# A spectral mixer and a gated feed-forward on one core: moving operands read alternately from their two halves

## The chip, the core and the metric

The kernel runs on one core of a Trainium2 chip. The metric is the device time of one execution in microseconds (us). The engines are named as the profile names them: PE is TensorE, the matrix engine; PEld is its weight load, which runs beside the matmuls; DVE is VectorE, ACT is ScalarE, POOL is GpSimd, SP is SyncE, which issues most DMAs. A matmul has a stationary operand (the weights, at most 128 x 128) and a moving operand, whose columns stream past the weights into PSUM. SBUF is the on-chip memory that both come from.

## What is computed

Two tensors are mixed by a gate: a spectral layer over 4096 tokens of width 640, and a gated feed-forward on the same tokens.

```python
x = A_x                                       # [2, 1, 4096, 640], fp32
g = sigmoid((x * gate_w).sum(-1, keepdims=True))
Xf = rfft2(x, axes=(1, 2))                    # over the 4096 tokens
z = Xf.reshape(B, H, Wf, 4, 160)              # four blocks of 160 channels
h = relu(z @ w1 + b1)                         # complex, by block
o = softshrink(h @ w2 + b2, 0.01)             # complex, by block
a = irfft2(o)
b = (gelu(x @ w_gate) * (x @ w_up)) @ w_down  # 640 -> 1728 -> 640
return g * a + (1 - g) * b
```

## The kernel before

All products run on PE in a 4-byte float format (fp32r) that carries part of a float's mantissa. Each float operand is therefore kept as two parts: `high` (L277) writes the rounded part with ACT, `low` (L280) the remainder with DVE, and a product takes three matmuls: high times high, high times low, low times high. A second transform of the spectral part (`fwd2`, L978) uses plain fp32 instead, which the profile records as two matmuls each.

The program goes through these stages, with one instruction order that is written out by hand for all engines:

- **Gate and up products** (`quad` L582, `deep_parts` L681, `plain` L730, `mixed` L762). Token tiles of 512 are the moving operand, in halves of 256 columns; weights of 128 x 128 are stationary. The products use a scheme with fewer multiplications (sums and differences of blocks), once for pairs and in part twice. All their matmuls go through `run` (L560, matmul on L562), through `go` in `deep_parts` (L694), or through L744 in `plain`. Between the products, hooks slip in the work of other stages: the first transform of the spectral part (`a_step`, L806, matmul on L817, 320 columns), the preparation of weights, and DMAs.
- **Spectral part.** For each chunk of 256 frequencies (one chunk has 258) and each of four blocks: `fwd2` makes the second step of the transform, `mlp1` (L1044) and `mlp2` (L1104) the two layers, `y_split` (L1129) and `inv1` (L1140) the first step of the way back. Its matmuls go through `mms` (L295, matmul on L297) and L1064 to L1066. In `mlp1` the moving operands are the transformed chunks `z`, `zs` and `zl` (256 columns), in `mlp2` the weights of the second layer (320 columns), in `inv1` the split output `ys` (320 columns).
- **Down product** (`down`, L1378), for 32 groups of tokens. The activations are stationary, the 640-wide weights are moving, 320 columns each. Its matmuls stand on L1406 (two products interleaved, `duo`) and on L562. `inv2` (L1351) makes the last step of the way back and feeds its result into the same output rows.

Every one of these matmuls loads new weights, so PEld has one record for each PE record. The addresses in SBUF come from pools with a fixed size for each kind of tile. Several tiles have gaps or offsets inside (`xs` in L518, `s2s` in L1299, `wx` in L1283).

The lines that the change touches are the matmuls themselves (L297, L562, L694, L744, L817, L1064 to L1066, L1406), the order of columns that `fwd2` writes to PSUM (L983) and what reads it (L984 to L1002), the shape of `y` in `mlp2` (L1110, L1124) and `y_split` (L1133, L1137), and the layouts that the host makes in `_tables` and `_layouts`. The rest of `quad` and `down` is the same in both kernels.

Of the kernel before, what the change touches and what calls it, by code (L numbers as in the profile page):

```python
# [15 lines left out]
P = 128  # L16
# [26 lines left out]
def _tables():  # L43
# [39 lines left out]
    f2 = np.concatenate([f2[0].reshape(P, P), f2[1].reshape(P, P), fny.reshape(P, 8)], axis=1)  # L83

    k2e = np.concatenate([np.arange(16), 31 - np.arange(16)])
    sig = np.concatenate([np.ones(16), -np.ones(16)])
# [128 lines left out]
def spectral_mix_kernel(ctx: ExitStack, tc: tile.TileContext, a):  # L215
# [79 lines left out]
    def mms(dst, ops):  # L295
        for i, (l, r) in enumerate(ops):
            nc.tensor.matmul(dst, l, r, start=i == 0, stop=i == len(ops) - 1)  # L297

# [258 lines left out]

    def run(dst, ops, first=True):  # L560
        for i, (l, r) in enumerate(ops):
            nc.tensor.matmul(dst, l, r, start=first and i == 0, stop=i == len(ops) - 1, skip_group_check=True)  # L562
            while inner and i == 1:
                inner.pop()()

# [115 lines left out]
    def deep_parts(gr, tp, t):  # L681
# [7 lines left out]
        def go(m, n, first, dst):  # L689
            if n not in b:  # L690
                b[n] = bank()
            acc = b[n][:, :256]
            for i, (l, r) in enumerate(prod([wa[m]], [xa[m]])):
                nc.tensor.matmul(acc, l, r, start=first and i == 0, stop=i == 2, skip_group_check=True)  # L694
            nc.vector.tensor_add(dst, acc, dst)

        def f0():
# [32 lines left out]
    def plain(key, t, hook):  # L730
# [3 lines left out]
        if t == 0:  # L734
            x = [x_of(o, *n, ("k4", q)) for q, n in enumerate((("b11", "b21"), ("b12", "b22")))]
            n = {}
            for q, ks, pause in ((0, (0, 1), (0, 1, 1)), (0, (2, 3), (5, 1, 0)), (0, (4,), (0,) * 3), (1, (4,), (0,) * 3),
                                 (1, (0, 1), (0,) * 3), (1, (2, 3), (0,) * 3)):
                for (a_, b_), z in zip(((0, 0), (1, 0), (0, 1)), pause):
                    warm(z)  # L740
                    for g, (dst, w) in enumerate(((pg, w0), (pu, w1))):
                        for i in ks:
                            m = n[q, g] = n.get((q, g), 0) + 1
                            nc.tensor.matmul(dst[:, 256 * q:256 * q + 256], w[:, i, a_], x[q][i][b_], start=m == 1,  # L744
                                             stop=m == 15, skip_group_check=True)
            for k in range(7):
                hook(k)
# [58 lines left out]
    def a_step(b, n2, h):  # L806
# [7 lines left out]
        for q in range(2):  # L814
            cs = slice(320 * q, 320 * q + 320)
            pa = bank()
            nc.tensor.matmul(pa[:, :320], f[:, h], xs[:, cs], start=True, stop=True)  # L817
# [160 lines left out]
    def fwd2(b, c, o, z, zs=None):  # L978

        pz = bank()  # L980
        for kp in range(4):
            ft = F2[0][:, 0:P] if (c == 0 and kp == 0) else F2[0][:, P:2 * P]
            nc.tensor.matmul(pz[:, kp * P:(kp + 1) * P], SC[b, c, kp][:, o:o + P], ft, start=True, stop=True)  # L983
        zz = [z[h][:, :, :CH].rearrange("p r (k f) -> p r k f", k=4) for h in range(2)]  # L984
        pr = pz.rearrange("p (k r f) -> p r k f", k=4, r=2)
        high(zz[0], pr)
        if zs:
            t = part_of(b, c, 0)
            t4 = t[:, :CH].rearrange("p (k f) -> p k f", k=4)
            nc.scalar.activation(t4, pr[:, 1], AF.Copy)  # L990
        low(zz[1], pr, zz[0])
        if zs:
# [1 line left out]
        if wide(b, c):  # L994
            pn = bank()
            for q in range(2):
                nc.tensor.matmul(pn[:, :4], SC[q, c, 0][:, o:o + P], fny[:, 4 * q:4 * q + 4], start=q == 0, stop=q == 1)
            split(z[0][:, :, CH:], z[1][:, :, CH:], pn[:, :4].rearrange("p (r f) -> p r f", r=2))
            if zs:
                nc.vector.tensor_copy(t[:, CH:], pn[:, :2])  # L1000
        F = width(b, c)
        return lambda: split(zs[0][:, :F], zs[1][:, :F], t[:, :F])  # L1002

    def rest(b, c):
# [39 lines left out]
    def mlp1(b, c, n, sums):  # L1044
# [15 lines left out]
        def last(dst):  # L1060

            for r in range(2):
                k = LAST1[r]
                nc.tensor.matmul(dst, w[:, k:k + P], z[0][:, r], start=r == 0, stop=False, skip_group_check=True)  # L1064
                nc.tensor.matmul(dst, w[:, k:k + P], z[1][:, r], start=False, stop=False, skip_group_check=True)  # L1065
            nc.tensor.matmul(dst, wl[:, 256:384], t1[:, n, :F], start=False, stop=True, skip_group_check=True)  # L1066
        h = two(b, c, "h")
        if wide(b, c):
            if n < 2:
# [34 lines left out]
    def mlp2(b, c, n):  # L1104
# [2 lines left out]
        q = n % 2  # L1107
        for j, (f0, M) in enumerate([(0, P), (P, P)] + ([(CH, 2)] if wide(b, c) else [])):
            if q == 0:
                Y[b, c, n // 2, j] = small([P, 2, 2, BS], name="y")  # L1110
            y = Y[b, c, n // 2, j]
            py = bank()
            fs = slice(f0, f0 + M)
# [1 line left out]
            for r in range(2):  # L1115
# [5 lines left out]

            m = small([P, 320], name="m")
            nc.scalar.activation(m[:M], py[:M, :320], AF.Relu, bias=neg2lam[:M])
            nc.vector.scalar_tensor_tensor(y[:M, :, q], py[:M, :320].rearrange("p (r o) -> p r o", r=2), 0.0,  # L1124
                                           m[:M].rearrange("p (r o) -> p r o", r=2), op0=OP.min, op1=OP.add)

    YS = {}

    def y_split(b, c, pb):  # L1129
        if wide(b, c):  # L1130
            t = NY[pb] = small([P, 2, 320], F32R, name="ny")
            nc.gpsimd.memset(t.bitcast(F32), 0.0)
            split(t[:2, 0], t[:2, 1], Y.pop((b, c, pb, 2))[:2, 0].rearrange("p n o -> p (n o)"))  # L1133
        for j in range(2):
            y = Y.pop((b, c, pb, j))
            t = YS[b, c, pb, j] = big([P, 2, 2, 320], F32R, name="ys")
            split(t[:, 0], t[:, 1], y.rearrange("p r n o -> p r (n o)"),  # L1137
                  nc.gpsimd if j == 1 and (b, c, pb) < (1, NCH - 2, 1) else nc.vector)

    def inv1(b, c, pb):  # L1140
# [237 lines left out]
    def down(i, u, hooks):  # L1378
# [18 lines left out]
        def duo(X, x, Y, y, hook, more=False):  # L1397
# [4 lines left out]
            for j, (p, q) in enumerate(zip(hx, hy)):  # L1402
                if j == 4:
                    hook()
                for k, op in ((0, p[0]), (0, p[1]), (1, q[0]), (0, p[2]), (1, q[-1]), *([(1, q[1])] if len(q) == 3 else ())):
                    nc.tensor.matmul((X, Y)[k], *op, start=n[k] == 0 and not (more and k), stop=n[k] == tot[k] - 1,  # L1406
                                     skip_group_check=True)
                    n[k] += 1

# [370 lines left out]
```

## Time and profile before

| | before |
|---|---|
| median of 3 runs | 2533.25 us (2531.83 to 2545.23) |
| span of the profiled execution | 2529.7 us |
| instructions in it | 54653 |
| PE records: L562 with 256 columns | 11196 |
| PE records: L1406 with 320 columns | 3844 |
| PE records of all kinds | 20239 |
| mean DMA rate over the span | 197 GB/s |

The profile comes from one execution. Its span runs from the first instruction to the last. The profile's page gives the busy time of each engine, the clock that the throttle granted to PE, the chain of work that ended last (followed back from the last instruction), and groups of equal instructions. Other views are cut from the same trace: busy time by windows of the span, with the number of instructions that start there; the chain in order of time, where one row is a run of equal instructions with its start, its length and its count; and the instructions of one engine in order of time, merged in rows of the same kind. Matmuls overlap, so the duration of one is longer than the distance from one to the next.

### The profile page before, as it was taken

What the parts mean: (1) busy time and instruction counts of PE and PEld (TensorE: products, weight loads), DVE (VectorE), ACT (ScalarE), POOL (GpSimd) and SP (SyncE); (2) the same over time, 40 slices, a digit from 0 to 9 for tenths busy, and PEclk for the clock granted to TensorE, in tenths of its full rate; (3) what the DMA queues carried; (4) which work ended last, traced back from release to release, by engine and by line L of the source; (5) the groups of instructions that cost most, each with busy time, mean ns of one, the idle gap of its engine ahead of it and who ended that gap; (6) DMA issues with size and microseconds to landing.
All of it is one profiled execution on the core that took longest, in us unless ns stands there. A gap on an engine that the chain in (4) does not pass through costs nothing.

```text
span 2529.7 us, 54653 instructions
## 1 busy us (share of the span) xinstructions
PE 2522.0 (100%) x20239; PEld 2516.3 (99%) x20239; DVE 2078.9 (82%) x4323; ACT 1492.6 (59%) x3503; POOL 387.3 (15%) x404
## 2 busy tenths in 40 slices
PE   9999999999999999999999999999999999999999
PEld 9999999999999999999999999999999999999999
DVE  7677788777777877787668788888999999899998
ACT  5455456656656666666556778787644444444443
POOL 0111100000000000000003111111133333333332
PEclk9999999999999999999999999999999999999999
DMA  6566666777777677777667455548744444444432
GB/s 216 203 214 229 224 224 211 245 234 241 234 251 236 220 235 243 237 239 227 217 228 220 130 164 142 161 144 270 289 142 147 157 157 140 133 152 157 154 131 102
DMA packets 351422, 499.50 MB, mean 197 GB/s; under 512 B 26028, under 2 KB 223276, under 8 KB 351156
## 3 DMA queue, kind: packets, MB, share of 16 engines
q1 hardware_dynamic: 333684, 445.02, 54.6%
q0 software_dynamic: 17472, 51.00, 5.5%
q8 instruction: 159, 2.61, 0.4%
q14 instruction: 107, 0.88, 0.1%
HBM read 307.10 MB, written 188.81 MB: 196 GB/s over the span
## 4 chain that ended last, share of the span: by engine, by line
PE 95%; DVE 2%; DMA 2%; ACT 1%; issue 0%; SPq 0%; DVEq 0%; ACTq 0%
PE bank L562 52%; PE bank L1406 22%; PE bank L297 14%; PE bank L983 3%; PE bank L694 2%; PE bank L817 1%; PE bank L1064 1%; PE bank L1065 1%; DMA xraw<-in_xT_dram 0%; DMA wdf<-wf 0%; PE bank L1066 0%; DMA scr<-as 0%; DMA zl<-zl 0%; DVE xo L281 0%; DMA wx<-wdf 0%
## 5 line engine op out<-in xcount | busy, mean ns | idle before, releaser
L562 PE MATMUL bank<-xo,w 128*128 128x256 f32 x11196 | 1319.4, 277 | 1.6 <-ACT u L588 0.6
L562 PEld LDWEIGHTS bank<-xo,w 128*128 128x128 f32 x11196 | 1298.0, 188 | 3.4 <-ACT u L588 1.2
L1406 PE MATMUL bank<-wx,ho 128*128 128x320 f32 x3844 | 560.7, 306 | 0.0
L1406 PEld LDWEIGHTS bank<-wx,ho 128*128 128x128 f32 x3844 | 557.2, 187 | 0.0
L281 DVE TENSOR_TENSOR ho<-hraw,ho 128x640 fp32r<-128x640 f32 (+3 forms) x384 | 260.8, 720 | 23.1 <-ACT ho L278 20.2
L588 ACT ACTIVATE u<-bank 128x256 f32<-128x256 f32 x328 | 125.5, 383 | 174.6 <-PE bank L562 166.4
L278 ACT ACTIVATE ho<-hraw 128x640 fp32r<-128x640 f32 x320 | 167.1, 571 | 97.7 <-PE bank L1406 74.9
L281 DVE TENSOR_TENSOR xs<-xr,xs 64x640 fp32r<-64x640 f32 x128 | 105.0, 820 | 75.8 <-ACT xs L278 73.6
L640 DVE TENSOR_TENSOR u<-bank,u 128x256 f32<-128x256 f32 x204 | 85.9, 421 | 86.4 <-ACT u L588 85.5
L281 DVE TENSOR_TENSOR xo<-xraw,xo 128x512 fp32r<-128x512 f32 x194 | 133.2, 687 | 16.4 <-ACT xo L278 15.1
L297 PE MATMUL bank<-wm,h 128*128 128x320 f32 (+1 forms) x792 | 137.6, 309 | 0.0
L819 DVE TENSOR_TENSOR as<-bank,as 64x320 f32<-64x320 f32 x256 | 113.9, 484 | 21.8 <-ACT as L818 20.1
L278 ACT ACTIVATE xo<-xraw 128x512 fp32r<-128x512 f32 x194 | 121.6, 627 | 6.1 <-DMA xraw<-in_xT_dram 4.9
L297 PEld LDWEIGHTS bank<-wm,h 128*128 128x128 f32 (+1 forms) x792 | 117.9, 185 | 1.3
L588 ACT ACTIVATE p<-bank 128x256 f32<-128x256 f32 x144 | 55.2, 383 | 105.8 <-DVE h L651 54.6
L562 PE MATMUL bank<-wx,ho 128*128 128x320 f32 x764 | 116.3, 307 | 0.0
L562 PEld LDWEIGHTS bank<-wx,ho 128*128 128x128 f32 x764 | 112.0, 188 | 0.0
L818 ACT ACTIVATE as<-bank 64x320 f32<-64x320 f32 x256 | 96.7, 426 | 23.8 <-PE bank L817 20.3
L278 ACT ACTIVATE xs<-xr 64x640 fp32r<-64x640 f32 x128 | 94.0, 734 | 22.9 <-DMA xr<-in_x_dram 21.1
L278 ACT ACTIVATE ho<-hs 128x640 fp32r<-128x640 f32 (+1 forms) x128 | 68.5, 570 | 61.5 <-DVE ho L281 42.1
L770 POOL MEMSET h<- 64x512 f32 x16 | 8.4, 523 | 624.9 <-PE bank L817 249.1
L1373 ACT ACTIVATE uu<-bank,gs 128x320 f32<-128x320 f32 x120 | 54.7, 524 | 76.5 <-PE bank L297 76.0
(196 smaller groups left out, 3961.8 us busy)
## 6 DMA issues: line engine op xcount, KB each, us to landing
xo<-xD SPq DMA_DIRECT2D x124, 512.0 KB
xraw<-in_xT_dram SPq DMA_DIRECT2D x215, 256.0 KB
hD<-h SPq DMA_DIRECT2D x184, 256.0 KB
hraw<-hD SPq DMA_DIRECT2D x128, 320.0 KB
xD<-xo POOLq DMA_DIRECT2D x64, 512.0 KB, 3.6
sc<-scr SPq DMA_DIRECT2D x65, 320.0 KB
xr<-in_x_dram SPq DMA_DIRECT2D x64, 320.0 KB
scr<-as SPq DMA_DIRECT2D x64, 320.0 KB
```

The lines of the kernel that those rows point to most:

```text
L278: nc.scalar.activation(dst, src, AF.Copy, scale=scale)
L281: eng.tensor_sub(dst, src, hi.bitcast(F32))
L297: nc.tensor.matmul(dst, l, r, start=i == 0, stop=i == len(ops) - 1)
L562: nc.tensor.matmul(dst, l, r, start=first and i == 0, stop=i == len(ops) - 1, skip_group_check=True)
L588: copy = lambda d, s_: nc.scalar.activation(d, s_, AF.Copy)
L640: nc.vector.tensor_add(u4, C, u4)
L694: nc.tensor.matmul(acc, l, r, start=first and i == 0, stop=i == 2, skip_group_check=True)
L818: nc.scalar.activation(stg[hi, cs], pa[lo, :320], AF.Copy)
L819: nc.vector.tensor_add(stg[hi, cs], pa[hi, :320], stg[hi, cs])
L983: nc.tensor.matmul(pz[:, kp * P:(kp + 1) * P], SC[b, c, kp][:, o:o + P], ft, start=True, stop=True)
L1373: nc.scalar.activation(uu[n2][:, cs], pe[:, :320], AF.Copy, scale=gs[:, b, 0, n2:n2 + 1])
L1406: nc.tensor.matmul((X, Y)[k], *op, start=n[k] == 0 and not (more and k), stop=n[k] == tot[k] - 1, skip_group_check=True)
```

## The change

Each fp32r moving operand with n columns is read in the order 0, n/2, 1, n/2+1, and so on. A helper gives the matmul a view of the same bytes with two steps:

```diff
+    def by_two(m):
+        return m.rearrange("p (k i) -> p i k", k=2)
...
     def mms(dst, ops):
         for i, (l, r) in enumerate(ops):
-            nc.tensor.matmul(dst, l, r, start=i == 0, stop=i == len(ops) - 1)
+            nc.tensor.matmul(dst, l, by_two(r), start=i == 0, stop=i == len(ops) - 1)
...
     def run(dst, ops, first=True):
         for i, (l, r) in enumerate(ops):
-            nc.tensor.matmul(dst, l, r, start=first and i == 0, stop=i == len(ops) - 1, skip_group_check=True)
+            nc.tensor.matmul(dst, l, by_two(r), start=first and i == 0, stop=i == len(ops) - 1, skip_group_check=True)
...
-            nc.tensor.matmul(pa[:, :320], f[:, h], xs[:, cs], start=True, stop=True)
+            nc.tensor.matmul(pa[:, :320], f[:, h], by_two(xs[:, cs]), start=True, stop=True)
...
-                for k, op in ((0, p[0]), (0, p[1]), (1, q[0]), (0, p[2]), (1, q[-1]), *([(1, q[1])] if len(q) == 3 else ())):
-                    nc.tensor.matmul((X, Y)[k], *op, start=n[k] == 0 and not (more and k), stop=n[k] == tot[k] - 1,
+                for k, (l, r) in ((0, p[0]), (0, p[1]), (1, q[0]), (0, p[2]), (1, q[-1]), *([(1, q[1])] if len(q) == 3 else ())):
+                    nc.tensor.matmul((X, Y)[k], l, by_two(r), start=n[k] == 0 and not (more and k), stop=n[k] == tot[k] - 1,
```

The matmuls on L694, L744 and L1064 to L1066 change in the same way. The warm-up matmuls at the start (L1516) and the plain fp32 ones (L983, L997) keep their moving order.

The results now come out in the alternated order, so the data are laid out to fit. On the host, `apart` puts the channels of the input, the token tiles, and the columns of the down weights in the order that the read undoes, and the columns of the second layer are permuted twice over, since its output is a moving operand again later. The columns of the second transform's table (`f2`) are reordered to match:

```diff
+    def apart(a, n):
+        return a.reshape(*a.shape[:-1], -1, n // 2, 2).swapaxes(-1, -2).reshape(a.shape)
+    perm = apart(perm, 320)
...
-    xp = xt.reshape(16, 2, 256, 5, P).transpose(0, 4, 1, 3, 2)
+    xp = apart(xt.reshape(16, 2, 256, 5, P).transpose(0, 4, 1, 3, 2), 256)
...
-    o["wd"] = c(A("B_w_down"))
+    o["wd"] = c(apart(A("B_w_down"), 320))
...
+    four = np.arange(BS).reshape(40, 2, 2).transpose(1, 2, 0).reshape(-1)
+    w2, b2 = w2[..., four], b2[..., four]
```

On the chip, `fwd2` writes its four products to PSUM in runs of 32 columns, so that the frequencies stand in the order that `mlp1` reads; and `mlp2` reads its result from PSUM with a step of two (real and imaginary parts alternate) and writes `y` in runs of 40:

```diff
-            nc.tensor.matmul(pz[:, kp * P:(kp + 1) * P], SC[b, c, kp][:, o:o + P], ft, start=True, stop=True)
-        zz = [z[h][:, :, :CH].rearrange("p r (k f) -> p r k f", k=4) for h in range(2)]
-        pr = pz.rearrange("p (k r f) -> p r k f", k=4, r=2)
+            nc.tensor.matmul(pz.rearrange("p (r e k f) -> p k r e f", r=2, e=2, k=4)[:, kp], SC[b, c, kp][:, o:o + P],
+                             ft.rearrange("p (r e f) -> p r e f", r=2, e=2), start=True, stop=True)
+        F = width(b, c)
+        if F > CH:
+            zz = [z[h][:, :, :F].rearrange("p r (e n) -> p r e n", e=2)[..., :P] for h in range(2)]
+            pr = pz.rearrange("p (r e n) -> p r e n", r=2, e=2)
+        else:
+            zz, pr = [z[h][:, :, :F] for h in range(2)], pz.rearrange("p (r n) -> p r n", r=2)
...
-                Y[b, c, n // 2, j] = small([P, 2, 2, BS], name="y")
+                Y[b, c, n // 2, j] = small([P, 2, 4, 2, 40], name="y")
...
-            nc.vector.scalar_tensor_tensor(y[:M, :, q], py[:M, :320].rearrange("p (r o) -> p r o", r=2), 0.0,
-                                           m[:M].rearrange("p (r o) -> p r o", r=2), op0=OP.min, op1=OP.add)
+            nc.vector.scalar_tensor_tensor(y[:M, :, :, q], py[:M, :320].rearrange("p (m n r) -> p r m n", m=4, r=2), 0.0,
+                                           m[:M].rearrange("p (m n r) -> p r m n", m=4, r=2), op0=OP.min, op1=OP.add)
```

No instruction is added, removed or moved on any engine. Only access patterns differ, and an access pattern shows in the order of instructions by its shape alone. On PE, in the spectral part, between the last matmuls of one `mlp1` and the sums of the next (`f` is the table of the second transform, `sc` its input, `wm` and `wl` the weights of the first layer, `z`, `zs` and `zl` its inputs), there stood before:

```order
L1066 MATMUL bank<-zl_20085,wl 128x256
L983 MATMUL bank<-f_19590,sc 128x128 x4
L997 MATMUL bank<-fny,sc 128x4 x2
L983 MATMUL bank<-f_19590,sc 128x128 x4
L297 MATMUL bank<-zs,wm 128x256 x3
L297 MATMUL bank<-z,wm 128x256 x3
```

At the same place there stands now:

```order
L1081 MATMUL bank<-zl_20085,wl 128x256
L993 MATMUL bank<-f_19590,sc 128x4x32 x4
L1012 MATMUL bank<-fny,sc 128x4 x2
L993 MATMUL bank<-f_19590,sc 128x4x32 x4
L307 MATMUL bank<-zs,wm 128x256 x3
L307 MATMUL bank<-z,wm 128x256 x3
```

The second transform's matmuls write four runs of 32 columns each; the others stand as they were, and their alternated reading is on the input side, which these rows don't print.

More of the change, by code (lines that the diff above doesn't have):

```diff
@@ L82, in _tables @@
     fny[:, 0, :, 0, 0] = fny[:, 0, :, 1, 1] = (-1.0) ** n2
-    f2 = np.concatenate([f2[0].reshape(P, P), f2[1].reshape(P, P), fny.reshape(P, 8)], axis=1)
+    f2 = [t.reshape(P, 2, 32, 2).transpose(0, 1, 3, 2).reshape(P, P) for t in f2]
+    f2 = np.concatenate([*f2, fny.reshape(P, 8)], axis=1)
     k2e = np.concatenate([np.arange(16), 31 - np.arange(16)])
@@ L693, in go @@
             for i, (l, r) in enumerate(prod([wa[m]], [xa[m]])):
-                nc.tensor.matmul(acc, l, r, start=first and i == 0, stop=i == 2, skip_group_check=True)
+                nc.tensor.matmul(acc, l, by_two(r), start=first and i == 0, stop=i == 2, skip_group_check=True)
             nc.vector.tensor_add(dst, acc, dst)
@@ L743, in plain @@
                             m = n[q, g] = n.get((q, g), 0) + 1
-                            nc.tensor.matmul(dst[:, 256 * q:256 * q + 256], w[:, i, a_], x[q][i][b_], start=m == 1,
+                            nc.tensor.matmul(dst[:, 256 * q:256 * q + 256], w[:, i, a_], by_two(x[q][i][b_]), start=m == 1,
                                              stop=m == 15, skip_group_check=True)
@@ L988, in fwd2 @@
             t = part_of(b, c, 0)
-            t4 = t[:, :CH].rearrange("p (k f) -> p k f", k=4)
+            t4 = t[:, :F].rearrange("p (e n) -> p e n", e=2)[..., :P] if F > CH else t[:, :F]
             nc.scalar.activation(t4, pr[:, 1], AF.Copy)
@@ L997, in fwd2 @@
                 nc.tensor.matmul(pn[:, :4], SC[q, c, 0][:, o:o + P], fny[:, 4 * q:4 * q + 4], start=q == 0, stop=q == 1)
-            split(z[0][:, :, CH:], z[1][:, :, CH:], pn[:, :4].rearrange("p (r f) -> p r f", r=2))
+            split(*(z[h][:, :, :F].rearrange("p r (e n) -> p r e n", e=2)[..., P] for h in range(2)),
+                  pn[:, :4].rearrange("p (r f) -> p r f", r=2))
             if zs:
-                nc.vector.tensor_copy(t[:, CH:], pn[:, :2])
-        F = width(b, c)
+                nc.vector.tensor_copy(t[:, :F].rearrange("p (e n) -> p e n", e=2)[..., P], pn[:, :2])
         return lambda: split(zs[0][:, :F], zs[1][:, :F], t[:, :F])
@@ L1063, in last @@
                 k = LAST1[r]
-                nc.tensor.matmul(dst, w[:, k:k + P], z[0][:, r], start=r == 0, stop=False, skip_group_check=True)
-                nc.tensor.matmul(dst, w[:, k:k + P], z[1][:, r], start=False, stop=False, skip_group_check=True)
-            nc.tensor.matmul(dst, wl[:, 256:384], t1[:, n, :F], start=False, stop=True, skip_group_check=True)
+                nc.tensor.matmul(dst, w[:, k:k + P], by_two(z[0][:, r, :F]), start=r == 0, stop=False, skip_group_check=True)
+                nc.tensor.matmul(dst, w[:, k:k + P], by_two(z[1][:, r, :F]), start=False, stop=False, skip_group_check=True)
+            nc.tensor.matmul(dst, wl[:, 256:384], by_two(t1[:, n, :F]), start=False, stop=True, skip_group_check=True)
         h = two(b, c, "h")
@@ L1132, in y_split @@
             nc.gpsimd.memset(t.bitcast(F32), 0.0)
[L1133 removed]
+            split(t[:2, 0], t[:2, 1], Y.pop((b, c, pb, 2))[:2, 0].rearrange("p m q n -> p (m q n)"))
         for j in range(2):
```

2 lines of the change are left out of this document (1 added, 1 removed).

## The prediction

> **What bounds the kernel now.** I read the page's busy shares first, then the busy times by stage, then the chain of work that ended last, and last the matmuls in order of time.
>
> ```profile
> PE 2522.0 (100%) x20239; PEld 2516.3 (99%) x20239; DVE 2078.9 (82%) x4323; ACT 1492.6 (59%) x3503; POOL 387.3 (15%) x404
> ...
> PEclk9999999999999999999999999999999999999999
> ...
> PE 95%; DVE 2%; DMA 2%; ACT 1%; issue 0%; SPq 0%; DVEq 0%; ACTq 0%
> ```
>
> TensorE is busy all the time, its clock is granted in full (a 9 means 90% or more; the windows below say 1.00), and the chain runs through it for 95% of the span. So there is no wait that could be removed. The time is the number of matmuls times the distance from one matmul to the next, and that distance is what this change can alter. The mean duration of one matmul in the groups (277 or 306 ns) is no use for it: matmuls overlap. The distance comes from runs of the chain, which hold a count and a length, and from windows.
>
> ```profile
> core 0: us, PE busy (x) PEld busy (x) DVE busy (x) ACT busy (x) POOL busy (x), PEclk, DMA share, GB/s
> 1830.00:2480.00 650.00, 650.00 (x4494) 650.00 (x4493) 618.67 (x1028) 307.30 (x662) 235.03 (x204) 1.00 0.44 148
> 1420.00:1770.00 350.00, 350.00 (x2715) 348.50 (x2715) 289.71 (x634) 276.67 (x656) 44.30 (x30) 1.00 0.59 173
> 30.00:1340.00 1310.00, 1308.74 (x11420) 1307.03 (x11419) 989.27 (x2285) 779.15 (x1874) 59.59 (x113) 1.00 0.70 230
> ```
>
> ```profile
> 141.68 22.78 PE bank L562 x201
> ...
> 1174.49 19.52 PE bank L562 x172
> ...
> 1826.25 17.91 PE bank L1406 x124
> 1848.81 17.91 PE bank L1406 x124
> ...
> 2505.22 17.79 PE bank L1406 x123
> ```
>
> The three windows are three stages: the gate and up products (30 to 1340 us, nearly all of 256 columns), the small matrices of the spectral part (1420 to 1770 us, both widths), and the down product (1830 to 2480 us, 320 columns only). A matmul of 256 columns takes 22.78/201 = 113.3 ns in its best runs. One of 320 columns takes 17.91/124 = 144.4 ns, and over the whole window 650/4494 = 144.6 ns. That second figure is a mean of unequal distances:
>
> ```profile
> 2250.22 0.59 PE L1406 MATMUL bank<-wx,ho 128*128 128x320 f32 x3
> 2250.36 0.60 PE L1406 MATMUL bank<-wx,ho 128*128 128x320 f32 x3
> 2250.51 0.60 PE L1406 MATMUL bank<-wx,ho 128*128 128x320 f32 x3
> 2250.66 0.59 PE L1406 MATMUL bank<-wx,ho 128*128 128x320 f32 x3
> 2250.80 0.60 PE L1406 MATMUL bank<-wx,ho 128*128 128x320 f32 x3
> ```
>
> These are five narrow windows, each row beginning with the first matmul in it. The starts are 0.14, 0.15, 0.15 and 0.14 us apart, though the instructions are alike and nothing waits. The short distance is 140 ns, the long one 145 to 150 ns. From 113.3 at 256 columns and 140 at 320, one column costs 26.7/64 = 0.417 ns; so the streaming is 106.7 or 133.3 ns, and each matmul pays a fixed 6.7 ns. What lies above 140 is a third part. It differs with the operands' places in SBUF, since nothing else differs between these matmuls. In the spectral part it is larger:
>
> ```profile
> 1449.19 0.52 PE L297 MATMUL bank<-z,wm 128*128 128x256 f32 x3
> 1449.55 0.39 PE L297 MATMUL bank<-zl,wl 128*128 128x256 f32 x2
> 1449.78 0.50 PE L297 MATMUL bank<-z,wm 128*128 128x256 f32 x3
> 1450.12 0.39 PE L297 MATMUL bank<-zl,wl 128*128 128x256 f32 x2
> ...
> 1450.91 1.04 PE L297 MATMUL bank<-wm,h 128*128 128x320 f32 x6
> 1451.79 0.46 PE L297 MATMUL bank<-wl,hl 128*128 128x320 f32 x2
> 1452.09 1.04 PE L297 MATMUL bank<-wm,h 128*128 128x320 f32 x6
> ```
>
> Eight matmuls of 256 columns start between 1449.19 and 1450.12, 116.3 ns apart, and eight of 320 between 1450.91 and 1452.09, 147.5 ns apart.
>
> **The change, part by part.**
>
> *The moving operand in alternating order.* The count of instructions and their order stay; each matmul of the fp32r kind reads the same bytes in another order. The trace of before has no moving operand with a step, so the price is bounded from both sides. Below: the best that streaming can do is to lose the third part, or the fixed part too, down to the weight load. Above: the streaming part could double, if each element opened a place of its own. The nearest row is the one with the smallest distance for its width, 113.3 and 140 ns. I take it that the third part goes and the fixed part stays. The reason: the third part depends on where one stream of addresses meets the next one and the weight load. A stream that is drawn from two places at half the rate each passes any one place half as often, so a meeting there should cost less. This is an argument, and no row proves it.
>
> Step by step: in the down stage 144.6 becomes 140, so 4.6 ns x 4494 = 20.7 us in the window, and 22 us over the stage's 697 us (from the chain's run at 1826.25 to the end of the one at 2505.22). In the spectral part and the first transform these groups count (shape, number, and behind the bar busy time and duration):
>
> ```profile
> L297 PE MATMUL bank<-wm,h 128*128 128x320 f32 x768 | 133.5, 309 | 0.0
> ...
> L297 PE MATMUL bank<-ys,i 128*128 128x320 f32 x392 | 62.9, 308 | 0.0
> L297 PE MATMUL bank<-z,wm 128*128 128x256 f32 x360 | 61.6, 279 | 0.0
> L817 PE MATMUL bank<-xs,f 128*128 128x320 f32 x256 | 58.3, 307 | 0.1
> L297 PE MATMUL bank<-wl,hl 128*128 128x320 f32 x248 | 57.2, 310 | 0.7 <-DVE hl L1100 0.7
> L297 PE MATMUL bank<-zl,wl 128*128 128x256 f32 x240 | 47.3, 278 | 0.0
> ...
> L1064 PE MATMUL bank<-z,wm 128*128 128x256 f32 x120 | 30.4, 277 | 0.0
> L1065 PE MATMUL bank<-z,wm 128*128 128x256 f32 x120 | 30.4, 277 | 0.0
> L1066 PE MATMUL bank<-zl,wl 128*128 128x256 f32 x60 | 16.7, 279 | 0.0
> ```
>
> The three L297 groups of 320 columns are 1408 matmuls at 147.5 ns: 7.5 x 1408 = 10.6 us. The 256 of the first transform (L817) may give the same 7.5 ns each, 1.9 us. The five groups of 256 columns are 900 matmuls that go from 116.3 to 113.3: 2.7 us. In the gate and up stage, 1308.74 us less 256 x 147.5 leaves 1271.0 for 11164 matmuls, 113.8 ns each, so 0.5 ns x 11164 = 5.6 us lie above the best runs; part of them are waits, and I take half, 2.8 us. Sum: 22 + 10.6 + 1.9 + 2.7 + 2.8 = 40 us.
>
> *Does something else become late?* In the down stage DVE is busy for 618.67 of 650 us. At 140 ns the window's matmuls last 629 us, still 10 us above DVE's work, so I charge nothing. If DVE's work cannot be packed that tightly, up to half of the 22 us stays. In the other two stages DVE and ACT have 17% or more to spare.
>
> *The weight load* is not changed, and it is the floor for 256 columns.
>
> ```profile
> 1381.82 0.97 PEld L983 LDWEIGHTS bank<-f,sc 128*128 128x128 f32 x8
> 1382.71 0.53 PEld L997 LDWEIGHTS bank<-fny,sc 128*128 128x128 f32 x4
> 1383.16 0.97 PEld L983 LDWEIGHTS bank<-f,sc 128*128 128x128 f32 x8
> ```
>
> Four of these loads stand beside matmuls of only 4 columns, and still twelve loads take 1.34 us, 111.7 ns each. So no reading order makes a 256-column matmul much shorter than 111.7 ns: at most 2.1 ns x 11164 = 24 us are in the largest stage.
>
> *The second transform's output order.* Its 320 fp32 matmuls (640 records) now write PSUM in runs of 32 columns instead of 128. They go at the pace of the weight load above, so a somewhat slower write hides behind it. Bounds: 0, and 640 x 111.7 ns = 71 us if each took double; I take 0, since runs of 32 are still contiguous.
>
> *The output of the second layer (L1124)* is read from PSUM with a step of two.
>
> ```profile
> L1124 DVE SCALAR_TENSOR_TENSOR y<-bank,m 128x320 f32<-128x320 f32 x128 | 58.9, 479 | 9.6 <-ACT m L1123 9.4
> ```
>
> If it doubled, DVE would have 59 us more, about as much as it has to spare in the spectral window alone (350 - 289.71 = 60 us), so PE hides nearly all of it; without that cover it would cost up to 59 us. The same holds for the chunk of 258 columns (some 70 matmuls). The host layouts move no work to the chip: the DMAs keep their sizes. I take 0 for all of these.
>
> The profiled execution has a span of 2529.7 us, 3.6 us below the median of 2533.25. So 2529.7 - 40 = 2489.7, and with the 3.6 around it **2493 us**.
>
> **A rule that speaks against it.** The rows show 113.3 and 140 ns for contiguous reads, and nothing for others. The Trainium skill, "SBUF — State Buffer", section "Specifications (TRN2)", says that SBUF is read in lines of 16 bytes, that full bandwidth needs at least two hits to a line, and that each crossing to a new line costs. In alternating order every fp32 element lies in another line than the one before it, so by that rule the streaming would slow down, by a factor that the section doesn't give; read as one step lost for each element it would make the time that of the last rival below, and by the rows it stays at the sum above. No run here shows it.
>
> **The rivals.**
>
> - *The fixed part goes as well.* For it: 6.7 ns after each matmul looks like the start of a new stream. Against it: the weights change at the same moment, and they are not touched. Price: 256 columns down to 111.7 ns, 24 us in the first stage and 4 us in the spectral part; 320 columns to 133.3 ns, 20 us in the spectral part and 3.6 in the first transform; in the down stage DVE becomes the bound at 618.67/650, which allows 34 us over 697. Together 86 us: 2448 us.
> - *The order does not matter.* The reader takes one column a step wherever it lies, and the third part comes from the weight load or from the first place alone, which stays. For it: PEld is as full as PE. Time 2533, at most some 5 us either way.
> - *The meetings become dearer.* Two places are opened at each start, so that every matmul pays as the spectral part's do now: 116.3 for 113.8 ns in the first stage is +28 us, 147.5 for 144.6 over 697/0.1446 = 4820 in the down stage is +14 us. Time 2575. It decides from any matmul on, for none of them has slack.
> - *The streaming doubles.* Each element opens a new place, and the reader holds only one open. It adds 106.7 ns to 11164 + 900 matmuls (1287 us) and 133.3 ns to 1408 + 256 and the down stage's 4820 (864 us), to a time near 4685 us. It decides as soon as a single place is held. For it: neighbours in the new order lie 512 or 640 bytes apart. Against it: nothing in the trace, which has no such read.
> - *The change does nothing*, if the two-step pattern were folded back into one: its elements are not contiguous, so it cannot be folded, and I give this no chance of its own.
>
> **How the numbers follow.** Forecast 0.45 (2493), fixed part too 0.13 (2448), no effect 0.14 (2533), dearer meetings 0.10 (2575), doubled 0.18 (4685). Leaving out the doubling, the range reaches from 2440 to 2585. Some 0.5%, 13 us, is what a measurement of this kernel tells from no change. Faster: 0.45 + 0.13 = 0.58; within: 0.14; slower: 0.10 + 0.18 = 0.28.
>
> **What would show it.** Right: runs of the down stage's chain of 124 matmuls in about 17.4 us instead of 17.91, and groups of 201 in the gate stage unchanged at 22.8. If those groups come down to 22.5, the fixed part goes too; if all runs grow by a constant per matmul, the meetings are dearer; if they grow in proportion to the columns, the streaming is hit. DVE idle time in the down stage should shrink while PE stays full; gaps in PE there would mean that DVE has become the bound. Wrong altogether: any matmul of 256 columns well above 120 ns.

## The result and the profile after

The changed kernel takes 2464.12 us (median of 4 runs, 2461.95 to 2466.74) against 2532.72 us (median of 4), a ratio of 0.9719 with a 95% interval of 0.969 to 0.9747: 2.8% faster, 69 us. The profiled execution has a span of 2465.0 us against 2529.7. Single executions of the kernel before lie between 2530.64 and 2545.23 us, so where a single run differs by some 15 us or less, the distances between matmuls decide and not the time.

The page of the changed kernel (busy time, share of the span and instructions of each engine, then the chain's shares):

```profile
PE 2445.0 (99%) x20239; PEld 2430.0 (99%) x20239; DVE 2065.8 (84%) x4323; ACT 1486.9 (60%) x3503; POOL 390.5 (16%) x404
...
PE 71%; DVE 19%; issue 5%; DMA 3%; ACT 2%; SPq 0%; DVEq 0%; ACTq 0%
```

The instructions are as many as before. PE is still busy almost throughout, but the chain now runs through DVE for 19% of the span, where it was 2%.

The windows of the changed kernel by stage (length, then busy time and number of instructions of each engine, clock, DMA):

```profile
30.00:1300.00 1270.00, 1267.07 (x11249) 1264.01 (x11248) 978.88 (x2261) 764.99 (x1843) 59.39 (x112) 1.00 0.71 233
1380.00:1720.00 340.00, 339.85 (x2756) 336.74 (x2755) 292.18 (x644) 276.11 (x668) 42.40 (x31) 1.00 0.58 169
1785.00:2410.00 625.00, 619.77 (x4523) 614.80 (x4522) 612.44 (x1034) 307.97 (x664) 241.91 (x206) 1.00 0.47 157
```

In the down stage 625 us hold 4523 matmuls, 138.2 ns each, where it was 144.6. DVE is busy for 612 of the 625 us. The clock is 1.00 in both kernels and plays no part.

Runs of the chain of the changed kernel (start, length, count):

```profile
140.62 22.45 PE bank L572 x201
...
1156.85 19.20 PE bank L572 x172
...
2074.71 16.84 PE bank L1421 x124
```

A matmul of 256 columns takes 22.45/201 = 111.7 ns, where it was 113.3 at best. One of 320 columns takes 16.84/124 = 135.8 ns; before, the mean in such a run was 144.4 and the best single distance 140. And the third part of the distance, the one that differed from matmul to matmul, is gone. Matmuls of the changed kernel in order of time, in the spectral part:

```profile
1426.70 0.50 PE L307 MATMUL bank<-z,wm 128*128 128x256 f32 x3
1427.03 0.39 PE L307 MATMUL bank<-zl,wl 128*128 128x256 f32 x2
1427.26 0.50 PE L307 MATMUL bank<-z,wm 128*128 128x256 f32 x3
1427.59 0.39 PE L307 MATMUL bank<-zl,wl 128*128 128x256 f32 x2
1427.81 0.28 PE L1079 MATMUL bank<-z,wm 128*128 128x256 f32 x1
...
1428.37 0.98 PE L307 MATMUL bank<-wm,h 128*128 128x320 f32 x6
1429.19 0.43 PE L307 MATMUL bank<-wl,hl 128*128 128x320 f32 x2
1429.46 0.98 PE L307 MATMUL bank<-wm,h 128*128 128x320 f32 x6
```

Ten matmuls of 256 columns start within 1.11 us, 111 ns each (116.3 before); eight of 320 within 1.09 us, 136 ns each (147.5 before). Different tiles, at different places, now have one distance.

Where the time came from follows from the first matmul of each stage: the first of L1064 (L1079 after the change) stands for the start of the spectral part, the first of L1406 (L1421) for that of the down stage. (Some work of a stage begins a little before its mark.) The rows of these lines (durations, then first and last start) in the kernel before:

```profile
L1064 PE MATMUL bank<-z,wm x128: 276/276/290, 1381.4 to 1790.0; 128*128 128x256 f32 x120, 128*128 128x258 f32 x8
L1406 PE MATMUL bank<-wx,ho x3844: 302/308/315, 1826.1 to 2522.8; 128*128 128x320 f32 x193
```

And in the changed kernel:

```profile
L1079 PE MATMUL bank<-z,wm x128: 275/275/277, 1361.6 to 1756.1; 128*128 128x256 f32 x120, 128*128 128x258 f32 x8
L1421 PE MATMUL bank<-wx,ho x3844: 299/299/403, 1792.2 to 2458.1; 128*128 128x320 f32 x193
```

| stage | before | after | saved |
|---|---|---|---|
| gate and up, to the first L1064 | 1381.4 us | 1361.6 us | 19.8 us |
| spectral part, to the first L1406 | 444.7 us | 430.6 us | 14.1 us |
| down, to the end of the span | 703.6 us | 672.8 us | 30.8 us |

All three stages gave something, 64.7 us in all.

### The profile page after: what moved, and what is told of

It is laid out like the page before. It is cut to its first block, busy times and chain, and to the rows that moved or that the text cites. A ratio compares the mean times of both kernels' runs of the same rounds, so it can differ in the third digit from the quotient of the medians.

```text
span 2465.0 us, 54653 instructions
## 1 busy us (share of the span) xinstructions
PE 2445.0 (99%) x20239; PEld 2430.0 (99%) x20239; DVE 2065.8 (84%) x4323; ACT 1486.9 (60%) x3503; POOL 390.5 (16%) x404
## 4 chain that ended last, share of the span: by engine, by line
PE 71%; DVE 19%; issue 5%; DMA 3%; ACT 2%; SPq 0%; DVEq 0%; ACTq 0%
PE bank L572 48%; PE bank L307 11%; DVE ho L288 7%; PE bank L1421 6%; DVE s2s L288 3%; PE bank L993 3%; DVE uu L1426 2%; PE bank L704 2%; DVE uu L1389 1%; PE bank L827 1%; DVE hs L1350 1%; DMA s<-scr 1%; PE bank L1079 0%; PE bank L1080 0%; DMA xraw<-in_xT_dram 0%
## 5 line engine op out<-in xcount | busy, mean ns | idle before, releaser
L572 PE MATMUL bank<-xo,w 128*128 128x256 f32 x11196 | 1298.3, 275 | 3.1 <-ACT u L598 1.5
L572 PEld LDWEIGHTS bank<-xo,w 128*128 128x128 f32 x11196 | 1276.1, 192 | 5.9 <-ACT u L598 2.1
L1421 PE MATMUL bank<-wx,ho 128*128 128x320 f32 x3844 | 532.4, 300 | 5.6 <-DVE ho L288 5.5
L1421 PEld LDWEIGHTS bank<-wx,ho 128*128 128x128 f32 x3844 | 524.4, 189 | 10.2 <-DVE ho L288 10.0
L288 DVE TENSOR_TENSOR ho<-hraw,ho 128x640 fp32r<-128x640 f32 (+3 forms) x384 | 226.8, 632 | 6.4 <-ACT ho L285 3.4
L288 DVE TENSOR_TENSOR xo<-xraw,xo 128x512 fp32r<-128x512 f32 x194 | 133.3, 688 | 17.0 <-ACT xo L285 15.7
L307 PE MATMUL bank<-wm,h 128*128 128x320 f32 (+1 forms) x792 | 129.7, 300 | 0.5 <-DVE h L1057 0.4
L288 DVE TENSOR_TENSOR s2s<-s,s2s 128x320 fp32r<-128x320 f32 x128 | 115.7, 963 | 2.4 <-ACT s2s L285 1.5
L307 PEld LDWEIGHTS bank<-wm,h 128*128 128x128 f32 (+1 forms) x792 | 111.8, 186 | 2.1 <-DVE h L1057 0.6
L572 PE MATMUL bank<-wx,ho 128*128 128x320 f32 x764 | 110.4, 300 | 0.9 <-DVE ho L288 0.9
L572 PEld LDWEIGHTS bank<-wx,ho 128*128 128x128 f32 x764 | 105.7, 189 | 2.1 <-DVE ho L288 2.1
L599 ACT ACTIVATE h<-bank 128x256 f32<-128x256 f32 x204 | 77.8, 381 | 29.4 <-PE bank L572 27.8
```

Source lines behind the costliest of these rows:

```text
L288: eng.tensor_sub(dst, src, hi.bitcast(F32))
L307: nc.tensor.matmul(dst, l, by_two(r), start=i == 0, stop=i == len(ops) - 1)
L572: nc.tensor.matmul(dst, l, by_two(r), start=first and i == 0, stop=i == len(ops) - 1, skip_group_check=True)
L599: gelu = lambda d, s_: nc.scalar.activation(d, s_, AF.Gelu_apprx_tanh)
L1421: nc.tensor.matmul((X, Y)[k], l, by_two(r), start=n[k] == 0 and not (more and k), stop=n[k] == tot[k] - 1, skip_group_check=True)
```

## The experiments

Single runs are compared by the spans of their profiles with 2465.0 us (changed) and 2529.7 us (before).

### One width at a time

```diff
     def by_two(m):
-        return m.rearrange("p (k i) -> p i k", k=2)
+        return m.rearrange("p (k i) -> p i k", k=2) if m.shape[-1] < 320 else m
```

> Only the moving operands of 256 and 258 columns are read alternately, those of 320 in plain order (their columns come out in another order, so channels are mixed up). Theory A (each start and each meeting of streams gets cheaper at either width): 256 columns go from 113.3-118 to 111.7 ns, 320 columns stay at 140-149, and the sum is 1.7 to 2 ns x 12,600 = 22-26 us, about 2508 us. Rival (the two widths help each other, or the 256 columns are bound by the weight load in both kernels and the gain is all in the 320 columns): about 2530 us.

The other run has `== 320` in place of `< 320`.

> Only the moving operands of 320 columns are read alternately, those of 256 and 258 in plain order (channels are mixed up as a result). Theory A: 320 columns at 135.8 ns instead of 144.6-147.5, which is 9 ns x 6700 = 60 us of matmul time, less some 15 us that DVE holds back in the down stage; about 2488 us, and the two halves of the change together give the 69 us of the whole. Rival (the gain lies in how widths follow each other): the 320 columns stay above 138 ns and the time is above 2505 us.

Both take about the same: 2506.25 us with the 256 columns alternated, 2506.39 us with the 320 columns, spans of 2504.5 and 2504.6 us. Each half gives 25 us of the 65. With the 256 columns alone it is as theory A says: 111.7 ns, and the 320 columns as before. The other half misses its forecast by 18 us. The 320 columns come down to 135.8 ns, but the 256 columns that stayed in plain order became dearer. The chain with only the 320 columns alternated:

```profile
141.59 22.78 PE bank L572 x201
...
336.66 17.68 PE bank L572 x156
354.61 3.06 PE bank L572 x26
...
823.33 20.26 PE bank L572 x172
```

And the spectral part's first matmul in the same kernel:

```profile
L1079 PE MATMUL bank<-z,wm x128: 276/276/290, 1400.0 to 1796.3; 128*128 128x256 f32 x120, 128*128 128x258 f32 x8
```

In the first 350 us, where no 320-column matmul stands between, the runs of 201 take 22.78 us as before. The first two matmuls of the first transform come at 354 us, and the pace changes right behind them, from 17.68/156 = 113.3 ns to 3.06/26 = 117.7 ns. Later, where they are mixed in throughout, the runs of 172 take 20.26/172 = 117.8 ns where it was 113.5, and the stage ends 18.6 us later than before (1400.0 against 1381.4). So a plain stream of 256 columns has at least two paces at the same places, 113.3 and about 118 ns, and which one it keeps depends on what ran before it. That is what the rival says of widths that follow each other, and it holds for this part: the widths are not independent. The rival's own numbers don't hold, since it had the 320 columns above 138 ns. Without that loss the two halves would make up the whole (25 + 25 + 18.6 = 69 against 65 us).

### What the place does in plain order

```diff
-            gap.extend([tiny([P, 1], name="gap"), pool.tile([P, 112], F32, name="gap", tag="gap", bufs=1)])
+            gap.extend([tiny([P, 1], name="gap"), pool.tile([P, 96], F32, name="gap", tag="gap", bufs=1)])
```

This is the kernel before with one tile 64 bytes smaller, so that the tiles behind it move down by 64 bytes.

> The kernel before, with its gap tile 64 bytes smaller, so that most moving operands of 256 columns (12,528 of them) start 64 bytes lower; nothing else changes, and nothing is left out. Theory P (in plain order the place of the moving operand against that of the weights sets the third part): 256 columns at 117 to 120 ns, as the few that start at such a place in the kernel before, so + 50 us, about 2580 us. Rival (the place is without effect, and the third part comes from what ran before): 2533 us.

It took 2595.8 us, 63 us more than before. The chain of this kernel:

```profile
145.58 23.85 PE bank L562 x201
...
1219.30 20.41 PE bank L562 x172
...
1927.81 18.17 PE bank L1406 x124
```

The 256 columns go from 113.3 to 118.7 ns and the 320 columns from 144.4 to 146.5 ns; the 50 us of the forecast had the 256 columns alone in them. So theory P holds: in plain order the price hangs on the place, and the kernel before stood at the better one of the two that were tried. In alternating order the matmuls of the spectral part and of the down stage, whose tiles lie at different places, have the one distance of 136 ns, as shown above. The changed kernel itself was not run with its tiles moved.

### How far apart the two places must lie

```diff
-        return m.rearrange("p (k i) -> p i k", k=2)
+        return m.rearrange("p (a k i) -> p a i k", k=2, i=16)
```

That is the form for places 16 columns (64 bytes) apart; with `i=8` they are 32 bytes apart, with `i=2` 8 bytes. The few operands of 258 columns stay as in the change in these and the following runs, except where the text on record says otherwise.

> The alternation stays, but between neighbouring pieces of 16 columns (64 bytes): 0, 16, 1, 17 and so on, then the next 32 columns; outputs come out permuted. Theory A (what counts is that each piece of 64 bytes is passed at half the rate): as the changed kernel, 111.7 and 135.8 ns, 2464 us. Rival B (the two places must be far apart, since neighbouring pieces are in each other's way): above 113 and 140 ns, 2530 us or more.

> The alternation goes on inside each piece of 16 columns (64 bytes): 0, 8, 1, 9 and so on; outputs come out permuted. Theory A (the unit is a piece of 64 bytes): both places lie in one piece, so it reads as the kernel before: 113.3 ns and 140 to 149 ns, about 2533 us. Rival C (the unit is 16 bytes, and it is the change of line at every element that helps): 111.7 and 135.8 ns, 2464 us.

> The alternation goes on inside each group of 4 columns (16 bytes): 0, 2, 1, 3, then the next four; outputs come out permuted. Theory D (a plain run with step one is fetched in pieces ahead of need, and that fetching collides with the weight load; any pattern whose innermost step is not one is read element by element and does not collide): 111.7 and 135.8 ns, 2464 us. Theory C (it is the change to another 16-byte line at each element that helps): as before, 2533 us, since both elements lie in one line.

The first two took 2464.64 and 2464.58 us, as the change itself. Neither the halves nor a distance matters, and the unit of 64 bytes in theory A falls: 32 bytes are enough. The third took 2529.92 us, as the kernel before. The chain with places 8 bytes apart:

```profile
141.53 22.78 PE bank L574 x201
...
1892.47 17.91 PE bank L1423 x124
```

These are the distances of plain order, 113.3 and 144.4 ns, though the innermost step isn't one. So theory D (any step other than one helps) falls. Theory C's unit, the line of 16 bytes, fits these runs, but they only bound it: 8 bytes apart are too near, and 32 bytes are enough. Places 16 bytes apart were not tried, so a unit of 32 bytes isn't ruled out.

### Other orders

```diff
-        return m.rearrange("p (k i) -> p i k", k=2)
+        return m.rearrange("p (i k) -> p k i", k=2)
```

> All even columns first, then all odd ones (step of 8 bytes, the 258-column ones stay as in the change); outputs come out permuted. Theory D: 111.7 and 135.8 ns, 2464 us. Theory C: two elements of a line follow each other, so half of the gain at most, 2500 us or more. Rule of the Trainium skill, 'SBUF - State Buffer', section 'Specifications (TRN2)' (two hits to a line suffice): no loss, as before, 2533 us.

With `"p (k i j) -> p i k j", k=2, j=4` runs of four columns come in turn from the two halves, with `j=2` runs of two, and with `"p (k i) -> p i k", k=16` single columns from sixteen places.

> Runs of 4 columns (16 bytes) are read in turn from the first and the second half: 0 to 3, n/2 to n/2+3, 4 to 7 and so on (258 columns plain); outputs come out permuted. Theory D: the innermost step is one, so the fetching in pieces is back, above 113 and 140 ns, 2533 us or more. Theory A' (two distant places at half the rate each are enough): 111.7 and 135.8 ns, 2464 us.

> Sixteen places are read in turn (columns 0, n/16, 2n/16 and so on; the 258-column ones from two); outputs come out permuted. Theory D: nothing is held open, so the number of places does not matter, 111.7 and 135.8 ns, 2464 us. Rival E (a few places are held open, two in the change): the streaming slows to about double, 4600 us.

> Runs of 2 columns (8 bytes) are read in turn from the first and the second half: 0, 1, n/2, n/2+1, 2, 3 and so on; outputs come out permuted. Model M (SBUF gives the moving side pieces of 8 bytes, one in two PE cycles, and the last two pieces are held) with cause F (pieces that follow each other must lie in different lines of 16 bytes, or the weight load gets in between): each piece is fetched once and the next lies elsewhere, so 111.7 and 135.8 ns, 2464 us. Cause G (a piece must be held over four columns, so that a late one is covered): here each piece is used up at once, so 113 and 140 ns or more, 2533 us or more.

The doubling with sixteen places is rival E's. For the rest no theory had the sizes; runs of four and runs of two fit open bounds alone (2533 us or more, of theory D, which has fallen, and of cause G). Even columns before odd ones took 4938.99 us, runs of four 2745.2 us, sixteen places 4993.15 us, runs of two 3589.1 us. From the chain, even before odd:

```profile
276.19 46.23 PE bank L574 x201
...
3647.05 35.27 PE bank L1423 x124
```

Sixteen places:

```profile
264.32 44.22 PE bank L572 x201
...
3580.38 38.58 PE bank L1421 x124
```

Runs of two:

```profile
201.90 33.50 PE bank L574 x201
...
2683.07 25.52 PE bank L1423 x124
```

Runs of four:

```profile
155.63 25.46 PE bank L574 x201
...
2046.21 19.02 PE bank L1423 x124
```

In one table, from the runs of 201 and of 124:

| order of the columns | 256 columns, ns | 320 columns, ns |
|---|---|---|
| plain; or 0, 2, 1, 3 in each four | 113.3 | 144.4 |
| from two places, 32 bytes or more apart | 111.7 | 135.8 |
| runs of 4 from two halves | 126.7 | 153.4 |
| runs of 2 from two halves | 166.7 | 205.8 |
| even, then odd | 230.0 | 284.4 |
| from sixteen places | 220.0 | 311.1 |

One picture fits the order of this table. Suppose the moving side reads through two readers that take turns, one the first, third, fifth element, the other the second, fourth, sixth. In plain order, and with 0, 2, 1, 3, each reader finds two of its elements in a row in a line of 16 bytes. From two places, each finds four. With even before odd, or with sixteen places, each finds one, and the streaming doubles: 230.0 is 116.7 more than 113.3, and the streaming part was 106.7. Runs of four leave two, with a jump after each; runs of two leave one, though the line comes back. The picture was made after these runs, and no run was made to test it. It doesn't give the size for runs of two, nor the 311 ns for 320 columns from sixteen places.

The rule of the Trainium skill, "SBUF — State Buffer", section "Specifications (TRN2)", asks for two hits to a line of 16 bytes. Taken for the stream as a whole it disagrees with the runs: even before odd has two hits to a line and pays double (230.0 ns), and the change, which takes every element from another line than the one before it, is faster than plain order (135.8 against 144.4 ns). Taken for each of two readers it fits the order of the table, and it doesn't tell that four hits are better than two (135.8 against 144.4 ns).

### What DVE holds back

```diff
-            split(h, l, raws[k // 2][:, 320 * (k % 2):320 * (k % 2) + 320])
+            high(h, raws[k // 2][:, 320 * (k % 2):320 * (k % 2) + 320])
+            high(l, raws[k // 2][:, 320 * (k % 2):320 * (k % 2) + 320])
```

> The changed kernel, with the low parts of the last transform's inputs written by ACT as copies of the high parts' source instead of DVE's differences (so that part of the computation is left out): DVE loses 120 instructions of 995 ns in the down stage, about 112 us, ACT gains 56 us. If DVE is what opens the gaps between PE's matmuls there, L1421's mean distance goes from 138.7 to 136 ns and the time falls by 12 to 15 us, to about 2450 us. Rival (the gaps come from DMAs or from ACT): 2464 us or more.

It took 2454.44 us, 10 us less than the changed kernel. Its windows in the down stage:

```profile
1785.00:2410.00 625.00, 624.55 (x4596) 624.07 (x4595) 569.42 (x933) 348.45 (x791) 232.49 (x209) 1.00 0.46 156
```

With 569 us of DVE work in place of 612, PE does 4596 matmuls in the 625 us in place of 4523, 136.0 ns each. So DVE is what opens the gaps in the down stage, and they cost about 10 us. DVE lost only 43 us in this window, though, where some 112 had been expected. The lines of the changed kernel in which DVE works there show why:

```profile
L288 DVE TENSOR_TENSOR s2s<-s,s2s 128x320 fp32r<-128x320 f32 x120 | 112.2, 995 | 1.2 <-ACT s2s L285 0.3
...
L1389 DVE SCALAR_TENSOR_TENSOR uu<-bank,gs,uu 128x320 f32<-128x320 f32 x116 | 55.7, 543 | 0.0
...
L288 DVE TENSOR_TENSOR ho<-hraw,ho 128x128 fp32r<-128x128 f32 x63 | 18.5, 294 | 0.0
```

A subtraction of 128x320 with both operands in SBUF takes 995 ns in the mean. Eight more fall in the spectral part, where POOL has little to do; DVE's groups of the kernel before in that part have the same instruction:

```profile
L281 DVE TENSOR_TENSOR s2s<-s,s2s 128x320 fp32r<-128x320 f32 x8 | 3.5, 486 | 0.5 <-ACT s2s L278 0.5
```

It takes 486 ns there. The trace of the changed kernel tells the two prices apart: in the down stage the 40 subtractions that overlap no POOL instruction take 487 ns (496 at most), the 80 that overlap one take 1248 ns in the mean (POOL's times in a profile are rough). An instruction of the same size that reads PSUM takes 543 ns (L1389), and those on L1426 that read PSUM take 538 ns with a POOL instruction beside them and 540 without. So the extra time goes with POOL's work and not with the subtraction, and without the subtractions another instruction has it, in the lines of the run above:

```profile
L288 DVE TENSOR_TENSOR ho<-hraw,ho 128x128 fp32r<-128x128 f32 x62 | 77.9, 1256 | 0.0
```

It took 294 ns in the changed kernel. The mean of 995 ns had suggested another order of the computation:

```diff
+        if c_seq[i][1]:
+            p, m_ = raws
+            nc.vector.tensor_add(p, p, m_)
+            nc.vector.scalar_tensor_tensor(m_, m_, -2.0, p, op0=OP.mult, op1=OP.add)
...
-            for n2, k in ((na, 0), (32 - na, 2)):
-                nc.scalar.activation(uu[n2][:, cs], pe[:, :320], AF.Copy, scale=gs[:, b, 0, n2:n2 + 1])
-                nc.vector.scalar_tensor_tensor(uu[n2][:, cs], po[:, :320], gs[:, b, k, n2:n2 + 1], uu[n2][:, cs],
-                                               op0=OP.mult, op1=OP.add)
+            for n2, pp in ((na, pe), (32 - na, po)):
+                nc.scalar.activation(uu[n2][:, cs], pp[:, :320], AF.Copy, scale=gs[:, b, 0, n2:n2 + 1])
```

> The changed kernel, with the sum and difference of the two parts of the last transform taken before the matmuls instead of behind them: for 30 of the 32 groups DVE loses 4 instructions of 543 ns that read PSUM and gains 2 of 820 to 995 ns, 0.2 to 0.5 us less per group of about 21 us. All of the computation is there. If DVE bounds the down stage, 5 to 15 us come back, 2450 to 2460 us. Rival (the two new instructions come at the head of the chain that PE waits for, or POOL holds them up): 2464 us or more.

It took 2503.04 us (ratio to the kernel before 0.989, interval 0.9873 to 0.9906), 39 us more than the changed kernel. The two new lines on DVE in the down stage:

```profile
L1316 DVE SCALAR_TENSOR_TENSOR s<-s,s 128x640 f32<-128x640 f32 x29 | 48.2, 1661 | 1.0
...
L1315 DVE TENSOR_TENSOR s<-s,s 128x640 f32<-128x640 f32 x29 | 35.1, 1209 | 1.9 <-DMA s<-scr 1.0
```

And the longest new waits of this kernel there (who waited for whom: total, times, longest):

```profile
ACT s2s L285 <- DVE s L1315: 72.5, 28, 3.9
...
DVE ho L288 <- ACT ho L285: 40.4, 29, 3.1
ACT s2s L285 <- DVE s L1316: 33.9, 28, 1.6
```

The pair takes 2870 ns, more than the four instructions it replaces (4 x 543 = 2172 ns), and ACT, which splits the results, waits for it and is late for `ho` behind it, for which DVE waits. Of the 58 new instructions the five that overlap no POOL instruction took 824 to 827 ns. The rival had both, the place in the chain and POOL. So no version here beats the changed kernel with its whole computation in place.

## Why the prediction was right, and where its sizes were off

The measured 2464 us lies in the range and on the forecast side; the forecast was 2493 us, and the first rival's 2448 us is nearer. By its own steps:

- **What bounds the kernel.** That the time is the number of matmuls times their distance held: the counts are the same, and the shorter distances give the gain of the three stages, less new gaps between matmuls (about 7 us in each of the first two stages and 12 in the down stage, summed from the starts in the traces).
- **The third part goes.** Right: it went in every stage. That the spectral part gave 14.1 us where the two terms for it gave 10.6 + 2.7 is luck, though. There 147.5 became 136 ns and 116.3 became 111, which is 16 + 5 = 21 us for the 1408 and 900 matmuls of the sum, and the new gaps took about 7 us back.
- **The fixed part stays.** This is the term that was mis-sized. It was taken as 6.7 ns and kept. By the prediction's own price of a column it fell to 135.8 - 133.3 = 2.5 ns for 320 columns, and 256 columns came down to the weight load's 111.7 ns. The first rival had that, with nothing left of the fixed part, and the signs that the prediction named say the same: runs of 124 in 16.84 us, not 17.4, and runs of 201 in 22.45, not 22.8. The Trainium skill, "TensorE: Matmul & The Clock Gate", section "Wait — 56ns, not 53.3ns?", gives N/2.4 + 2.5 ns for N columns and matmuls that follow each other; worked out from it, an estimate for 320 columns is 135.8 ns, and the traces agree in alternating order (135.8) and not in plain order (140 at best).
- **The gate and up stage** carries most of the miss: 2.8 + 1.9 us were summed, 19.8 us came. A change of 1.7 ns in the mean, over more than 11,000 matmuls, had been filed under the rival alone.
- **The down stage** gave 30.8 us where 22 were summed. At 135.8 ns it would have given some 10 us more, and DVE kept them. The sum had charged nothing for DVE, on the ground that 629 us of matmuls would still cover 619 us of DVE work. At 140 ns that might have stood; at 136 it doesn't (612 busy of 625 us, and 10 us back when its work was cut).
- **The weight load as a floor**: 111.7 ns was worked out, 111.7 ns is what 256 columns now take in the long runs of the chain, such as those of 201 and 172.
- **Edits taken at nothing.** The second transform's eight records between two `L307` rows take 0.81 us in the changed kernel (1425.47 to 1426.28 us in order of time) and 0.80 us before (1447.95 to 1448.75), so the runs of 32 columns in PSUM cost nothing. The instruction that reads PSUM with a step of two (now L1139) takes 481 ns in the median, 473 before.
- **The reason given for the forecast** (a stream from two places passes any one place half as often) fits the result but isn't shown. From 32 bytes up the distance of the places doesn't matter; that 8 bytes are too near, and that a price hangs on what ran before and not on the place alone, it didn't have.
- **The rivals.** No effect and dearer meetings are out. The doubling was a real danger, not of this order but of its neighbours: two of the orders that were tried pay it.

## What to carry to other kernels

When PE is full and its clock granted in full, compare the distance between matmuls (length over count in a run of the chain) with the floor of the weight load and with the columns times the price of one column; what is left over can lie in how the moving operand is read. An fp32r moving operand read in turn from two places, 32 bytes or more apart, lost most of that remainder at every place that it had in this kernel, while plain order depended on a 64-byte shift and on the matmuls before. When DVE instructions on SBUF look dear, look at which of them overlap POOL's work, before moving them. Try an order on the whole kernel without mending the layouts first, since its neighbours can double the time.

## What was not expected of the hardware

- One order of the same bytes made a 256-column matmul 230.0 ns and another 111.7 ns, with PE busy for 99% of the span or more in both kernels.
- One tile 64 bytes smaller, which shifts the tiles behind it, cost 63 us of 2533 in plain order.
- Plain streams of 256 columns kept one of at least two paces (113.3 or about 118 ns) at the same places, by what had run before. Why a pace is kept is open, and so is why two places help at all: the two readers are a guess.
- DVE subtractions of 128x320 with both operands in SBUF took 487 ns apart from POOL's instructions and 1248 ns in the mean beside them; DVE instructions of that size with an operand in PSUM were no slower beside POOL (538 against 540 ns). When the subtractions were left out, the extra time moved to another DVE instruction. No run took POOL's work away.
